# Two temporaries of the gates' exponential placed in a PSUM bank, with a newly derived instruction list

## The chip, the cores and the metric

The kernel runs on one core of a Trainium2 chip. The metric is device time in microseconds (us) of one launch, taken as the median of several runs. A core has five engines that run side by side, each strictly in its own order: TensorE (PE in the profile; its weight loads are PEld), VectorE (DVE), ScalarE (ACT), GpSimd (POOL) and SyncE (SP), which here only starts DMAs. Its two near memories are SBUF and PSUM; PSUM has eight banks of 512 float32 values in each of 128 partitions.

## The reference, cut to what matters

Two layers, one after the other. The first is a gated recurrent attention (4 batches, 8 heads, 768 steps, head size 40). Per step and head, with the running maximum `m`:

```python
m_new  = np.maximum(f_gate[t] + m, i_gate[t])
f_stab = np.exp(f_gate[t] + m - m_new)
i_stab = np.exp(i_gate[t] - m_new)
C = f_stab * C + i_stab * outer(v[t], k[t]);  n = f_stab * n + i_stab * k[t]
y[t] = sigmoid(o_gate[t]) * (C @ q[t]) / max(|n . q[t]|, 1)
```

The second is a feed-forward layer on the 3072 rows of 320 values that come out: `h = x @ w_in` (2048 columns), `g = (a0 + a1 h + a2 h^2 + a3 h^3) / (1 + |b0||h| + |b1| h^2 + 1e-6)`, `g @ w_out`. Everything is float32.

## The kernel before, in words

**The work.** Attention is cut into 24 units (6 blocks of 128 steps by 4 batches). A unit `u` loads k, q, v (`lk_u`, `lq_u`, `lv_u`), scales k by the input gate (`kp_u`, POOL), transposes k and q on TensorE (`tk_u`, `tq_u`) with copies back on ACT (`ek_u`, `eq_u`), forms the decays by a scan (`sc_u`, DVE), multiplies q by them (`qa_u`, DVE for the first ten units), and makes the score products `S_u`, the masked scores `P_u` (two DVE multiplies), the new state `ow_u`, and the state updates `u0_u`, `u1_u` (DVE). Two units make a pair `m`, whose outputs are `it_m`, `i1_m` (TensorE), `ab_m`, `rc_m`, `g_m`, `x_m`, then transposes `xt_m` and splits into a high and a low part (`xh_m` ACT, `xl_m` DVE).

The feed-forward layer runs over 12 blocks `n` of 256 rows by 8 steps `i` of 256 hidden columns. Step `n_i` is: `f1` (16 matmuls into a PSUM tile `ph`), `ha`, `p1`, `u`, `y`, `r0` (ACT), `p3`, `gh`, `m`, `gl` (DVE), `w`, `rm` (POOL), `f2` and `f3` (matmuls into `po`; `f2` needs `gh`, `f3` needs `gl`). In the trace `gh` writes the tile gH, `gl` writes gL, `m` writes w, `p3` writes p, `sc` writes e, `u0` writes sm, `u1` writes st, `P` writes pm. The weights come as 32-bit words, loaded by `raw_i*`, `raw_j*`, `raw_o*` and split on ACT (`s0`, `s2`, `o0`), DVE (`s1`, `s3`; tiles lo0i, zi, lo1o, zo and the like) and POOL (`o2`). The first two blocks run in two halves of four steps each.

**The gates.** All input and forget gates are turned into factors by an exponential that is built from arithmetic on DVE (`exp`, lines 461 to 484): a clamp, a scaling with rounding, a subtraction, two reductions, a polynomial of degree six, a shift of the exponent, a mask and a last product. A small part for the first 256 steps is done early (`early`). The rest (`gates`, lines 561 to 662) is one pass over tiles of 128 partitions by 256 values, named gate_x in the trace. Its operations carry the list names gate.7 to gate.20: gate.7 the clamp, gate.8 and gate.9 the scaling and the subtraction, gate.10 and gate.11 the reductions, gate.12 the first and gate.13 to gate.17 the other steps of the polynomial, gate.18 the shift, gate.19 the mask, gate.20 the product. All of their temporaries (t, n, r, p) lie in SBUF. Afterwards gate.22 (TensorE, tile pi), gate.24, gate.25 and some DMAs bring the factors to the units from the third block of steps on.

**The order.** The text `ORDER` (lines 147 to 309) lists every operation by name, `name.k` being the k-th operation of that name. `_Plan.listed` and `_Plan.issue` issue the operations in this order, so each engine and the DMA queue of SP run in the order in which their own operations stand there. Six of the eight PSUM banks form a ring "h" (`BANKS = 6`), which `ph`, the transposes (kq, px), scores (ps), outputs (y), states (ow) and the weights' lo tiles share; a new tile takes a bank when all users of an older tile are through. The 90 operations `hot` are matmuls whose result nobody reads; both lists have all of them ahead of f2_0_0.

Of the kernel before, what the change touches and what calls it, by code (L numbers as in the profile page):

```python
# [159 lines left out]
o2_j0 o2_j0.1 hot.68 S_1 P_1 P_1.1 s1_o3 gate.9 s3_o3.1 o2_j1.1 pf_2 ogl_1 ogl_3 og_0 ow_1 u0_1 s3_o3 gate.10 sc_2  # L160
it_0 it_0.1 i1_0 hot.69 ab_0 ab_0.1 rc_0 raw_i2 s0_i2 d1_1 u1_1 s1_i2 hot.70 hot.71 s2_i2 g_0 x_0 raw_i0 s2_i0 s0_i0
raw_i1 lk_2 gate.11 s3_i2 g_0.1 hot.72 hot.73 hot.74 hot.75 hot.76 gate.12 kp_2 raw_o2 pa_3 hot.77 hot.78 x_0.1 s0_i1
pc_3 s1_i0 hot.79 hot.80 xt_0 o0_i2 hot.81 lq_2 oc_j0 lk_3 o2_i2 s3_i0 hot.82 hot.83 hot.84 tk_2 o0_o3 lq_3 xh_0 s1_i1
o0_i0 o2_i0 lv_2 xh_0.1 xl_0 xl_0.1 gate.13 ek_2 s0_o2 s1_o2 gate.18 s2_i1 hot.85 hot.86 hot.87 hot.88 ke_2 kp_3 s3_i1
hot.89 lk_4 tq_2 s2_o2 s0_o2.1 s3_o2 eq_2 o0_i1 qa_2 s1_o2.1 f1_0_0 f1_0_0.1 S_2 tk_3 P_2 gate.14 P_2.1 pf_3 raw_i3
gate ow_2 ha_0_0 p1_0_0 u_0_0 raw_i7 ek_3 tq_3 p3_0_0 s3_o2.1 oc_j1 sc_3 o2_o3 o2_i1 w_0_0 y_0_0 lv_3 f1_0_1 eq_3
gate.19 raw_i5 u0_2 lq_4 lf_4 gate.1 d1_2 gate.15 gate.16 u1_2 qa_3 o0_o2 f1_0_1.1 S_3 ke_3 P_3 r0_0_0 gh_0_0 P_3.1
ha_0_1 s0_i3 f2_0_0 f2_0_0.1 s2_i3 u_0_1 f1_0_2 s1_i3 lq_5 o2_o2 s0_i7 m_0_0 kp_4 s3_i3 f1_0_2.1 p1_0_1 s1_i7 p3_0_1
ow_3 s2_i7 s3_i7 o0_i3 w_0_1 y_0_1 r0_0_1 rm_0_0 lk_5 gl_0_0 it_1 it_1.1 u0_3 i1_1 ha_0_2 u_0_2 o2_i3 gh_0_1 m_0_1
d1_3 u1_3 f1_0_3 f1_0_3.1 w_0_2 ab_1 ab_1.1 p1_0_2 rc_1 s0_i5 p3_0_2 f3_0_0 s2_i5 s1_i5 ha_0_3 p1_0_3 f3_0_0.1 g_1 x_1  # L170
rm_0_1 s3_i5 tk_4 ek_4 y_0_2 f2_0_1 gl_0_1 f2_0_1.1 u_0_3 g_1.1 x_1.1 xt_1 sc_4 xh_1 w_0_3 p3_0_3 tq_4 eq_4 xh_1.1
ke_4 kp_5 xl_1 xl_1.1 f3_0_1 f3_0_1.1 S_4 r0_0_2 o0_i5 raw_o4 gate.17 P_4 y_0_3 r0_0_3 o2_i5 P_4.1 f1_1_0 gh_0_2
gh_0_3 m_0_2 m_0_3 tk_5 ek_5 f1_1_0.1 ha_1_0 la_4 qa_4 s0_o4 s2_o4 s1_o4 rm_0_2 f1_1_1 o0_i7 s3_o4 gl_0_2 lv_4 lf_5
rm_0_3 sc_5 gl_0_3 s0_o4.1 u_1_0 f2_0_2 f2_0_2.1 f1_1_1.1 w_1_0 s1_o4.1 p1_1_0 ha_1_1 tq_5 p3_1_0 raw_o7 ow_4 la_5
# [5 lines left out]
f2_1_1.1 gate.20 gh_1_3 ha_0_4 ek_6 s0_o6.1 f3_1_1 f3_1_1.1 s1_o6.1 f2_1_2 f1_0_5 o0_o4 u_0_4 p1_0_4 m_1_3 gl_1_2  # L180
f1_0_5.1 lf_7 s0_o6 ha_0_5 f2_1_2.1 la_6 g_2.1 x_2.1 tq_6 s1_o6 s3_o6.1 gate.24 rm_1_3 gl_1_3 w_0_4 u_0_5 f3_1_2
f3_1_2.1 f2_1_3 w_0_5 p1_0_5 eq_6 f1_0_6 o2_o4 s3_o6 o0_o6 f1_0_6.1 p3_0_4 y_0_4 r0_0_4 o2_o6 ha_0_6 gate.25 p3_0_5
y_0_5 S_6 qa_6 P_6 f2_1_3.1 f3_1_3 f3_1_3.1 r0_0_5 lk_7 pe_1_3 s0_o7.1 pe_1_3.1 u_0_6 lv_6 lv_7 f1_0_7 f1_0_7.1 P_6.1
gh_0_4 m_0_4 rm_0_4 ha_0_7 p1_0_6 ogl_10 f2_0_4 f1_1_4 u_0_7 gh_0_5 w_0_6 m_0_5 gl_0_4 f2_0_4.1 f3_0_4 f3_0_4.1
gate.22 f2_0_5 f1_1_4.1 s1_o7.1 p3_0_6 p1_0_7 y_0_6 s3_o7.1 p3_0_7 r0_0_6 rm_0_5 gl_0_5 gate.23 o0_o7 ha_1_4 w_0_7
kp_7 f2_0_5.1 f3_0_5 xt_2 o2_o7 f3_0_5.1 gh_0_6 m_0_6 xh_2 xl_2 lq_8 gate.26 y_0_7 r0_0_7 lk_8 tk_7 f2_0_6 rm_0_6
f2_0_6.1 u_1_4 w_1_4 ek_7 f1_1_5 f1_1_5.1 f1_1_6 gh_0_7 m_0_7 gl_0_6 p1_1_4 xh_2.1 f3_0_6 p3_1_4 xl_2.1 ha_1_5 sc_7
u_1_5 y_1_4 rm_0_7 gl_0_7 f3_0_6.1 p1_1_5 r0_1_4 gh_1_4 ogl_8 ogl_6 la_7 ogl_9 lf_8 lk_9 ogl_11 ke_7 ogl_7 f2_0_7
f2_0_7.1 p3_1_5 m_1_4 f1_1_6.1 ha_1_6 u_1_6 tq_7 f1_1_7 w_1_5 w_1_6 rm_1_4 y_1_5 p1_1_6 f3_0_7 f3_0_7.1 ev_0_7
ev_0_7.1 r0_1_5 f1_1_7.1 f1_2_0 p3_1_6 gh_1_5 y_1_6 r0_1_6 ha_1_7 gate.27 f2_1_4 f2_1_4.1 m_1_5 lq_9 gl_1_4 f1_2_0.1  # L190
eq_7 f3_1_4 qa_7 f3_1_4.1 f2_1_5 ed_0_7 rm_1_5 gl_1_5 S_7 P_7 ow_6 kp_8 f2_1_5.1 d0_6 f3_1_5 tk_8 P_7.1 lk_10 p1_1_7
p3_1_7 u_1_7 gh_1_6 m_1_6 ha_2_0 u_2_0 p1_2_0 f1_2_1 f3_1_5.1 f2_1_6 p3_2_0 u0_6 w_1_7 y_1_7 r0_1_7 w_2_0 f2_1_6.1
f1_2_1.1 rm_1_6 ek_8 y_2_0 gh_1_7 d1_6 u1_6 m_1_7 d0_7 gl_1_6 rm_1_7 ow_7 u0_7 r0_2_0 it_3 it_3.1 gh_2_0 og_6 d1_7
u1_7 la_8 ogl_16 sc_8 i1_3 tq_8 ab_3 ha_2_1 m_2_0 gl_1_7 ab_3.1 p1_2_1 rm_2_0 p3_2_1 f3_1_6 f3_1_6.1 f2_1_7 u_2_1 rc_3
# [10 lines left out]
u_3_0 la_10 ed_1_7.1 lq_11 lv_10 gate.28 p3_3_0 xt_4 S_10 xh_4 P_10 f2_2_6.1 y_2_7 r0_2_7 xl_4 P_10.1 xh_4.1 f3_2_6
f3_2_6.1 gh_2_7 f1_3_1 w_3_0 kp_11 y_3_0 r0_3_0 f1_3_1.1 ha_3_1 xl_4.1 tk_11 m_2_7 gh_3_0 m_3_0 f1_3_2 f1_3_2.1 qa_10
ek_11 tq_11 f2_2_7 f2_2_7.1 rm_2_7 rm_3_0 gl_2_7 p1_3_1 u_3_1 ha_3_2 f3_2_7 f3_2_7.1 ow_10 eq_11 lq_12 lf_11 S_11
p3_3_1 w_3_1 gl_3_0 u_3_2 ev_2_7 ev_2_7.1 sc_11 ke_11 y_3_1 r0_3_1 gh_3_1 d0_10 P_11 u0_10 p1_3_2 lv_11 p3_3_2 m_3_1
f1_3_3 f1_3_3.1 ha_3_3 u_3_3 f2_3_0 p1_3_3 P_11.1 f2_3_0.1 f3_3_0 w_3_2 f3_3_0.1 f2_3_1 la_11 lf_12 kp_12 w_3_3 d1_10
# [1254 lines left out]
```

## Time and profile before

| | us |
|---|---|
| median of 3 runs (lowest, highest) | 518.59 (517.47, 518.70) |
| the profiled execution, its own time | 516.0 |
| span of its trace, first to last instruction | 514.1 |
| TensorE busy | 483.4 |
| VectorE busy | 429.8 |
| ScalarE busy | 403.7 |
| GpSimd busy | 382.6 |

Busy times are sums over the whole span. [...] What ended an engine's idle time stands in brackets behind an instruction of the timeline. An instruction that is held up after it has started shows as a long one, not as idle time.

### The profile page before, as it was taken

The numbers are of one execution on the slowest core, as the hardware profiler recorded it, in microseconds if no ns is written. First come the engines' busy times: TensorE is split into PE (matmuls) and PEld (weight loads), VectorE is DVE, ScalarE is ACT, GpSimd is POOL, SyncE is SP. The second block draws the span as 40 slices with busy tenths as digits, with TensorE's granted clock in tenths as the row PEclk, the third lists the DMA queues.
The fourth block names the chain that finished last, engine by engine and source line by source line (L and its number), as shares of the span: only waits on it lengthen the run. The fifth ranks groups of instructions, "written<-read, shape, count | busy, mean of one in ns | idle before, by whom it ended". The sixth has DMA issues, their size and how long they took to land.

```text
span 514.1 us, 14184 instructions
## 1 busy us (share of the span) xinstructions
PE 483.4 (94%) x5631; PEld 466.0 (91%) x5631; DVE 429.8 (84%) x716; ACT 403.7 (79%) x698; POOL 382.6 (74%) x365
## 2 busy tenths in 40 slices
...
GB/s 177 186 181 251 213 145 211 52 53 108 61 128 51 52 102 102 80 77 79 83 30 143 108 52 71 82 35 42 46 62 81 1 74 1 18 12 2 27 1 33
DMA packets 119439, 42.55 MB, mean 83 GB/s; under 512 B 103618, under 2 KB 111874, under 8 KB 119362
## 3 DMA queue, kind: packets, MB, share of 16 engines
...
q14 instruction: 31, 0.25, 0.2%
q10 hardware_dynamic: 130, 0.16, 0.1%
...
## 4 chain that ended last, share of the span: by engine, by line
PE 71%; DVE 9%; DMA 4%; issue 4%; ACT 4%; POOL 3%; SPq 2%; DVEq 0%; ACTq 0%; POOLq 0%
PE ph L34 28%; PE po L34 27%; PE y L34 4%; PE kq L34 3%; PE ow L34 3%; PE ps L34 3%; DVE w L34 2%; SPq L34 2%; DMA rawi<-in_moe_w_in_dram 2%; POOL p L34 2%; DVE gH L34 2%; PE px L34 1%; DMA qn<-in_q_dram 1%; PE hot L34 1%; DVE gL L34 1%
## 5 line engine op out<-in xcount | busy, mean ns | idle before, releaser
L34 POOL TENSOR_TENSOR p<-p,w 128x512 f32<-128x512 f32 (+1 forms) x97 | 126.6, 1305 | 63.4 <-DVE w L34 60.4
L34 PE MATMUL ph<-xk,wi 128*128 128x256 f32 x1152 | 169.4, 283 | 0.6 <-DVE pm L34 0.3
L34 PEld LDWEIGHTS ph<-xk,wi 128*128 128x128 f32 x1152 | 151.0, 190 | 2.4 <-issue 0.6
L34 PE MATMUL po<-wo,gH 128*128 128x320 f32 x768 | 136.6, 314 | 4.4 <-DVE gH L34 4.4
L34 POOL TENSOR_TENSOR w<-w,ha 128x512 f32<-128x512 f32 (+1 forms) x97 | 128.6, 1330 | 14.0 <-ACT w L34 13.8
L34 PEld LDWEIGHTS po<-wo,gH 128*128 128x128 f32 x768 | 116.7, 190 | 5.4 <-DVE gH L34 4.6
L34 DVE SCALAR_TENSOR_TENSOR w<-w,gH 128x512 f32<-128x512 f32 (+1 forms) x97 | 85.0, 877 | 4.5 <-POOL gt L34 0.5
L34 DVE SCALAR_TENSOR_TENSOR gL<-p,ps,ph 128x512 fp32r<-128x512 f32 (+1 forms) x97 | 71.1, 733 | 18.9 <-POOL p L34 16.7
L34 ACT ACTIVATE ph<-w,cd 128x512 f32<-128x512 f32 (+1 forms) x97 | 66.5, 687 | 23.4 <-POOL w L34 10.9
L34 DVE SCALAR_TENSOR_TENSOR gH<-p,ps,ph 128x512 fp32r<-128x512 f32 (+1 forms) x97 | 71.3, 735 | 14.7 <-ACT ph L34 12.3
L34 ACT ACTIVATE w<-ha,ba 128x512 f32<-128x512 f32 (+1 forms) x97 | 78.6, 811 | 3.1
L34 PE MATMUL po<-wo,gL 128*128 128x320 f32 x384 | 78.5, 317 | 1.1 <-DVE gL L34 1.1
L34 DVE SCALAR_TENSOR_TENSOR p<-p,ps,ph 128x512 f32<-128x512 f32 (+1 forms) x97 | 70.4, 734 | 9.9 <-ACT p L34 9.5
L34 ACT ACTIVATE ha<-ph 128x512 f32<-128x512 f32 (+1 forms) x97 | 57.6, 593 | 26.8 <-PE ph L34 25.8
L34 ACT ACTIVATE p<-ph,ps 128x512 f32<-128x512 f32 (+1 forms) x97 | 65.3, 677 | 1.5 <-DVE gL L34 1.4
L34 PEld LDWEIGHTS po<-wo,gL 128*128 128x128 f32 x384 | 59.7, 189 | 3.2 <-DVE gL L34 2.5
L34 ACT ACTIVATE ph<-ph 128x512 f32<-128x512 f32 (+1 forms) x97 | 56.1, 579 | 2.2
L34 PE MATMUL ph<-xk,wY 128*128 128x256 f32 x192 | 53.8, 280 | 0.0
L34 PE MATMUL ph<-xk,wj 128*128 128x256 f32 x192 | 53.7, 280 | 0.0
L34 PEld LDWEIGHTS ph<-xk,wj 128*128 128x128 f32 x192 | 36.4, 190 | 0.0
L34 PEld LDWEIGHTS ph<-xk,wY 128*128 128x128 f32 x192 | 36.4, 189 | 0.0
L34 PE MATMUL hot<-ident 128*128 128x128 f32 x180 | 24.8, 292 | 4.0 <-DVE flag_out L369 4.0
...
## 6 DMA issues: line engine op xcount, KB each, us to landing
...
```

Source lines behind the costliest of these rows:

```text
L34: made = fn(*args, **kwargs)
```

## The change

In `gates`, the temporaries n and p of the exponential move from SBUF into one PSUM bank of the ring "h", in columns 0 to 255 and 256 to 511. The bank is taken at gate.8, the first to write n, and comes free after gate.20, the last to read p. `exp` takes these two as functions, so that the tile is made when the first operation is issued; `early` keeps its SBUF temporaries.

```diff
     def exp(step, tiles, to=None, w=None):
-        x, t, m, r, p = tiles.values()
+        x, t, m_, r, p_ = tiles.values()
+        m, p = (z if callable(z) else lambda z=z: z for z in (m_, p_))
...
-        step(lambda: V.tensor_scalar(p, m, MAGIC, None, op0=ALU.subtract), r=[gm], w=[gp], cost=0.4)
+        step(lambda: V.tensor_scalar(p(), m(), MAGIC, None, op0=ALU.subtract), r=[gm], w=[gp], cost=0.4)
...
-        work = dict(zip(("gB.t", "gB.n", "gB.r", "gB.p"), work))
+        def bank(j):
+            if "gP" not in G:
+                G["gP"] = ring(psH, "h", [P, 512], "gP")
+            return G["gP"][:, j * 2 * SQ : (j + 1) * 2 * SQ]
+        work = {"gB.t": work[0], "gP.n": lambda: bank(0), "gB.r": work[2], "gP.p": lambda: bank(1)}
...
         def step(fn, cost=0.59, engine="DVE", w=(), r=(), **kw):
+            if "gP.n" in w:
+                kw["new"] = [("gP", ("h", BANKS))]
             plan.add("gate", engine, cost, fn, r=r, w=w, **kw)
```

The list has the same 2723 words in another order. It is the same up to word 150, and TensorE's order is the same again from f1_0_6 on, apart from a few places late in the list. Two stretches of DVE's own order, without what is left out at "...":

```
before: gate.7 s1_o3.1 gate.8 P_1 P_1.1 s1_o3 gate.9 ... gate.10 sc_2 ... gate.11 s3_i2 gate.12 ... gate.13 s1_o2 gate.18
        ... P_2 gate.14 P_2.1 p3_0_0 s3_o2.1 sc_3 gate.19 u0_2 gate.15 gate.16 u1_2 qa_3 P_3 gh_0_0 ... gate.17 ... gate.20
after:  ... P_1 P_1.1 qa_1 sc_2 u0_1 u1_1 ... qa_2 ... P_2 P_2.1 ... sc_3 gate.7 u1_2 p3_0_0 P_3 P_3.1 s1_i3 s3_i3 u0_3 qa_3
        gh_0_0 ... s3_o7 gate.8 gate.9 gate.10 gl_0_2 u0_4 sc_5 gate.11 qa_5 u1_4 gh_0_3 p3_1_0 P_5 P_5.1 gate.12 m_0_3 gate.18
        gate.13 gh_1_0 u0_5 m_1_0 gl_0_3 gate.14 u1_5 gate.15 p3_1_1 gl_1_0 gate.16 sc_6 ... gate.19 ... gate.17 ... gate.20
```

And of TensorE's and the DMA queue's:

```
PE before: f1_0_0 f1_0_0.1 S_2 tk_3 pf_3 ow_2 tq_3 f1_0_1 f1_0_1.1 S_3 f2_0_0 f2_0_0.1 f1_0_2 f1_0_2.1 ow_3 it_1 it_1.1 i1_1
PE after:  S_2 hot.84 f1_0_0 ... tk_3 ow_2 pf_3 tq_3 pa_3 S_3 f1_0_1 ow_3 it_1 it_1.1 i1_1 f1_0_1.1 f2_0_0 f2_0_0.1 tk_4 f1_0_2
SP before: ... lk_4 raw_i3 gate raw_i7 oc_j1 lv_3 raw_i5 lq_4 lf_4 gate.1 lq_5 lk_5 raw_o4 la_4 lv_4
SP after:  ... gate lv_2 lq_3 raw_i3 lv_3 lk_4 oc_j1 raw_i7 raw_o4 gate.1 lf_4 lq_4 raw_i5 lf_5 la_4
```

## Rows read from the trace of the kernel before

**Rows 1.** Windows, all engines: stretch, length, busy per engine, granted clock, DMA

```profile
40.00:60.00 20.00, 18.84 (x320) 17.26 (x320) 19.29 (x39) 18.09 (x33) 14.51 (x16) 1.00 1.00 242
...
80.00:100.00 20.00, 18.42 (x262) 17.08 (x262) 19.86 (x32) 16.19 (x30) 15.81 (x16) 0.98 0.51 110
...
120.00:460.00 340.00, 339.41 (x3970) 330.34 (x3969) 285.51 (x448) 278.74 (x477) 272.11 (x252) 1.00 0.30 66
```

**Rows 2.** Timeline of PE, 64 to 72 and 94 to 102 us

```profile
64.30 2.50 PE L34 MATMUL po<-wo,gH 128*128 128x320 f32 x8 [4.44 <-DVE gH L34]
66.60 1.48 PE L34 MATMUL ph<-xk,wi 128*128 128x256 f32 x6
...
68.30 0.88 PE L34 MATMUL ph<-xk,wi 128*128 128x256 f32 x6
...
69.34 0.79 PE L34 MATMUL ow<-vb,pm 128*64 128x82 f32 x16
...
71.80 0.96 PE L34 MATMUL ph<-xk,wi 128*128 128x256 f32 x6
...
82.71 1.33 PE L34 MATMUL po<-wo,gH 128*128 128x320 f32 x8
...
96.88 0.79 PE L34 MATMUL y<-vb,pm 128*64 128x82 f32 x16 [1.58 <-DVE gL L34]
...
99.83 1.62 PE L34 MATMUL ph<-xk,wi 128*128 128x256 f32 x6
```

**Rows 3.** Windows, same columns, where the clock fell

```profile
64.00:66.00 2.00, 1.70 (x6) 1.70 (x7) 2.00 (x4) 2.00 (x4) 1.29 (x1) 0.50 0.87 147
...
100.00:102.00 2.00, 2.00 (x10) 2.00 (x11) 1.97 (x6) 1.53 (x3) 2.00 (x3) 0.50 0.68 113
```

**Rows 4.** Timeline of DVE, 57 to 64 us

```profile
57.98 0.40 DVE L34 SCALAR_TENSOR_TENSOR gate_x<-gate_x 128x256 f32<-128x256 f32 x1
58.30 0.32 DVE L34 COPY sm<-ow 104x164 f32<-104x164 f32 x1
58.54 3.88 DVE L34 SCALAR_TENSOR_TENSOR gate_x<-gate_x 128x256 f32<-128x256 f32 x2
62.34 0.31 DVE L34 TENSOR_TENSOR st<-tm,ow 104x164 f32<-104x164 f32 x1
...
63.51 0.73 DVE L34 SCALAR_TENSOR_TENSOR gH<-p,ps,ph 128x512 fp32r<-128x512 f32 x1
```

**Rows 5.** Timeline of POOL and then of ACT, same stretch

```profile
58.70 0.58 POOL L34 TENSOR_TENSOR tm<-sm,ab 104x164 f32<-104x164 f32 x1 [2.02 <-DVE sm L34]
...
61.42 0.72 POOL L34 TENSOR_TENSOR kp<-kr,inat 128x320 f32<-128x320 f32 x1
...
62.69 0.63 ACT L34 ACTIVATE lo0i<-rawi 128x512 int32<-128x512 uint8 x1 [1.96 <-DVE st L34]
```

**Rows 6.** Instructions that touch gate_x: duration ns min/median/max, first and last start

```profile
L34 DVE SCALAR_TENSOR_TENSOR gate_x<-gate_x x9: 396/478/3437, 41.8 to 103.5; 128x256 f32<-128x256 f32 x9
L34 DVE TENSOR_SCALAR gate_x<-gate_x x5: 283/367/735, 37.9 to 51.4; 128x256 f32<-128x256 f32 x4, 128x256 int32<-128x256 int32 x1
L34 PE MATMUL pi<-ident,gate_x x2: 272/272/273, 119.7 to 119.9; 128*64 128x128 f32 x2
```

**Rows 7.** Groups of DVE by shape, 0 to 130 us: busy, mean ns

```profile
L34 DVE SCALAR_TENSOR_TENSOR gate_x<-gate_x 128x256 f32<-128x256 f32 x9 | 8.4, 937 | 0.1
L34 DVE SCALAR_TENSOR_TENSOR w<-w,gH 128x512 f32<-128x512 f32 x12 | 11.7, 983 | 0.4
L34 DVE SCALAR_TENSOR_TENSOR lo0i<-rawi,lo0i 128x512 int32<-128x512 int32 x8 | 5.5, 689 | 1.3 <-ACT lo0i L34 1.3
L34 DVE SCALAR_TENSOR_TENSOR lo1o<-rawo,lo1o 128x320 int32<-128x320 int32 x8 | 3.9, 488 | 1.3 <-ACT lo1o L34 1.1
L34 DVE TENSOR_TENSOR pm<-ps,e 128x256 f32<-128x256 f32 x14 | 5.5, 414 | 0.4 <-PE ps L34 0.4
```

**Rows 8.** Chain of waits, 57 to 64 us: start, length, what

```profile
57.76 4.60 DMA qn<-in_q_dram
```

More of the change, by code (lines that the diff above doesn't have):

```diff
@@ L160 @@
[L160 to L174, printed above, removed]
@@ L180 @@
[L180 to L194, printed above, removed]
@@ L205 @@
[L205 to L209, printed above, removed]
@@ new lines @@
+hot.83 xl_0.1 o2_i0 o2_j0.1 o0_i2 s2_o3 ke_2 S_2 hot.84 P_2 f1_0_0 f1_0_0.1 raw_o2 s0_o3 P_2.1 s2_o2 o2_i2 s1_o3 s3_o3
+s3_i1 hot.85 hot.86 hot.87 lk_3 kp_3 gate s0_o2.1 s0_o2 s1_o2.1 s1_o2 s3_o2 s0_o3.1 hot.88 hot.89 o0_i1 ha_0_0 o2_i1
+s1_o3.1 tk_3 ek_3 u_0_0 lv_2 ow_2 pf_3 s3_o2.1 u0_2 d1_2 s3_o3.1 w_0_0 sc_3 gate.7 ke_3 u1_2 o0_o2 lq_3 p1_0_0 tq_3
+o2_o2 eq_3 pa_3 p3_0_0 raw_i3 s2_i3 pc_3 S_3 P_3 P_3.1 s0_i3 s1_i3 s3_i3 lv_3 lk_4 f1_0_1 ow_3 u0_3 d1_3 kp_4 qa_3
+oc_j1 raw_i7 it_1 it_1.1 y_0_0 r0_0_0 gh_0_0 m_0_0 s2_i7 s0_i7 i1_1 ab_1 s1_i7 o0_i3 ab_1.1 f1_0_1.1 ha_0_1 u_0_1
@@ new lines @@
+p1_0_1 rm_0_0 raw_o4 rc_1 g_1 s3_i7 u1_3 gate.1 gl_0_0 f2_0_0 s2_o4 p3_0_1 w_0_1 lf_4 sc_4 s0_o4 s1_o4 o0_o3 x_1 o2_i3
+g_1.1 y_0_1 r0_0_1 gh_0_1 f2_0_0.1 tk_4 f1_0_2 f3_0_0 ek_4 f3_0_0.1 f1_0_2.1 s3_o4 m_0_1 rm_0_1 ke_4 lq_4 raw_i5 s0_i5
+ha_0_2 lf_5 s1_i5 s2_i5 x_1.1 u_0_2 s3_i5 w_0_2 gl_0_1 la_4 tq_4 eq_4 la_5 f1_0_3 qa_4 p1_0_2 f1_0_3.1 ha_0_3 xt_1
+lk_5 kp_5 f2_0_1 S_4 p1_0_3 p3_0_2 p3_0_3 xh_1 o2_o3 u_0_3 y_0_2 d0_4 raw_o7 lq_5 w_0_3 f2_0_1.1 P_4 xl_1 P_4.1 xh_1.1
+xl_1.1 tk_5 f3_0_1 r0_0_2 gh_0_2 s0_o7 f3_0_1.1 s1_o7 s2_o7 ek_5 o0_i5 f1_1_0 f1_1_0.1 m_0_2 lv_4 rm_0_2 s3_o7 f1_1_1
@@ new lines @@
+ow_4 gate.8 gate.9 gate.10 gl_0_2 u0_4 sc_5 gate.11 ha_1_0 p1_1_0 y_0_3 o2_i5 d1_4 u_1_0 lv_5 ke_5 w_1_0 tq_5 eq_5
+qa_5 f1_1_1.1 r0_0_3 f2_0_2 f2_0_2.1 u1_4 gh_0_3 ha_1_1 u_1_1 f3_0_2 S_5 w_1_1 p3_1_0 f3_0_2.1 o0_i7 P_5 P_5.1 gate.12
+ow_5 y_1_0 r0_1_0 m_0_3 gate.18 gate.13 gh_1_0 d0_5 u0_5 rm_0_3 m_1_0 f2_0_3 f1_1_2 raw_o6 s2_o6 p1_1_1 f1_1_2.1
+ha_1_2 gl_0_3 gate.14 d1_5 u1_5 f2_0_3.1 u_1_2 f3_0_3 gate.15 p3_1_1 y_1_1 rm_1_0 gl_1_0 gate.16 it_2 p1_1_2 it_2.1
+i1_2 ab_2 ab_2.1 r0_1_1 f3_0_3.1 f1_1_3 lk_6 lf_6 sc_6 f1_1_3.1 pe_0_3 pe_0_3.1 rc_2 w_1_2 f2_1_0 f2_1_0.1 gh_1_1
```

112 lines of the change are left out of this document (66 added, 46 removed).

## The prediction

> **What bounds the kernel now.** I first read the windows: from 120 to 460 us TensorE is busy 339.4 of 340 us at full clock, while the other engines have a sixth or more to spare [rows 1]. What happens there is paid for by TensorE's work alone, and the change touches no matmul. So the time can only move where TensorE still loses time, ahead of about 120 us, or at the end, where the order stays nearly as it is. Ahead of 120 us two engines press: the DMAs up to about 60 us (mean busy share 1.00, 242 GB/s in 40 to 60 us), and DVE (19.3 of 20 us busy there, and 19.9 of 20 in 80 to 100 us) [rows 1].
>
> Next I read TensorE's timeline for its holes. The largest is before the first `po` at 64.30 us: 4.44 us idle, ended by DVE's gH. [...] That is 1.2 + 0.6 = 1.8 us more, so this one hole costs 6.2 us. A second one stands at 96.88 us: 1.58 us idle, again ended by DVE, and a window at 0.50 of the clock behind it (2 us at half speed, 1.0 lost) [rows 2, 3]: 2.6 us.
>
> Then DVE's timeline ahead of that gH. Two exponential instructions take 3.88 us together; by the list of the tile's instructions the longest one takes 3.44 us, the shortest of the same shape 0.40 [rows 4, 6]. In the same time POOL runs four multiplications and subtractions without a hole, from 58.70 to 62.14 us [rows 5]. The DVE instruction, with both inputs in SBUF, ends when POOL's string ends. Behind it `st`, `qA`, `pm` and gH run without a break, and ACT too waits 1.96 us for that `st` [rows 4, 5].
>
> The point from which both lists run alike on TensorE is past by the two `pi` transposes (gate.22), at 119.7 us [rows 6]. The work ahead of it is the same set of operations in both; so the change is worth what those transposes come earlier or later.
>
> **The exponential itself.** Of its nine SCALAR_TENSOR_TENSOR instructions eight now have one input in PSUM; gate.19 keeps two in SBUF (it is the 0.40 us one at 57.98) [rows 4]. The nine take 9 x 0.937 = 8.4 us, the eight 8.0 [rows 7]. With one PSUM input the same size is to be seen in `pm` (0.414 us), and `lo1o`, which also writes PSUM, takes 0.488 for 320 columns, 0.689 for 512, so 1.05 ns a column and 0.42 for 256 [rows 7]. Eight at 0.42 are 3.4: 4.6 us less. The lower bound of the saving is 3.0 us (the 3.44 us instruction alone), the upper one 8.0 - 8 x 0.40 = 4.8. The four TENSOR_SCALARs that move (gate.8, 9, 12, 18) now take 0.28 to 0.74, median 0.37 [rows 6]; none with such a shape in PSUM stands in the trace, so I bound each by 0.28 and 0.49 (`lo1o`, larger) and take 0.42, nearest to `pm`: 0.2 us more in all at the median, up to 0.3 less against the collided one. I count it at zero.
>
> [...]
>
> **The stall and the order.** 3.0 us of TensorE's 4.44 us hole is that one instruction. The rest is cover by order: the new list puts ow_3, it_1 and i1_1 ahead of f2_0_0, work that in the trace takes from 69.34 to 71.80 us, 2.5 us [rows 2]. All of these need v of unit 3, whose load is moved ahead of raw_i7 and of oc_j1 in SP's queue. At the same time gate.8 to gate.16 leave the stretch ahead of gh_0_0. So I expect f2_0_0 to find gH ready, or nearly, and the whole 6.2 us to go (bounds: 3.0 if the rest of the hole and the slow clock stay, 6.2).
>
> **What is given back.** The gates have not gone; eleven of them (gate.8 to 16, 18, 19) now stand on DVE between gh_0_0 and gh_0_4, where only gate.17 and gate.20 stood, and DVE is the pressed engine there (19.9 of 20 us in one window) [rows 1]. An instruction of 0.40 to 0.42 us lets the next start after 0.32 (57.98 to 58.30 us) [rows 4], at 0.42 by the same overlap after 0.34, so the eleven take 3.7 to 4.6 us (without the overlap). In exchange P_3.1, s1_i3, s3_i3 and u0_3 (0.4 + 0.69 + 0.69 + 0.3 us by their kinds, 1.8 with the overlap) come ahead of gh_0_0 [rows 4, 7]. Net 1.9 to 2.5, I take 2.3. Behind each gate waits whatever DVE has next, the gH and gL on which f2 and f3 wait. In the trace before, the gates ran up to 62 us beside a DMA stage at a share of 1.00, where they filled DVE; that cover is gone, and this is the price of it.
>
> The sum: 6.2 - 2.3 = 3.9 us less. The profiled execution lasted 516.0 us (span 514.1, 1.9 around it) and would go to 512.1; the median of the runs is 518.6, 2.6 above it, and goes to 514.7. DVE's own account comes near: 4.6 us less collision over the whole start. The two small shifts of order late in the list (among others f1_9_3 behind f3_8_7, la_22 ahead of lq_22) I cost at nothing, since TensorE has other work on both sides; a hole there would cost its length.
>
> **The rivals.** (a) *The bank is missed.* One of six banks is away from gate.8 to gate.20. Counted in the lists from each tile's first to last user, at the places 540 to 599 all six are claimed at 41 of 60, before at 11 of 60. If an `f1` must wait for a bank that comes free by a gL that stands late on DVE, TensorE gets a hole as at 59.9 us with the slow clock behind it: 6.2 us, and the time is 514.7 + 6.2 = 520.9, slower. It decides from 3.9 us of such waits on; one hole like that at 96.88 (2.6 us) leaves 517.3. For it: DVE is that full, and both holes of the trace ended by DVE [rows 2]. Against: the list was made with the bank counted, and ranks an `f1` only behind the last user of the bank that it takes.
>
> (b) *Nothing that counts is won.* The chain of waits lays 4.60 us up to 62.36 us on a q load, not on DVE [rows 8]; if the DMAs at a share of 1.00 are the true bound up to 62 us, a freed DVE waits there, and the gates come on top later. Or the collisions go elsewhere: `w<-w,gH` with both inputs in SBUF takes 0.983 us in the mean where `lo0i` of the same columns takes 0.689 [rows 7], and POOL's work is no less. The time is 518.6 give or take 1.5. Against: the 3.44 us instruction uses nothing of q, and POOL's string ends with it [rows 5, 6]. [...]
>
> (c) *More is won.* With DVE freed of 4.6 us, the second hole closes too: another 2.6 us, 512.1. For it: it also waits for DVE. Against: the gates now stand just there.
>
> **How the numbers follow.** Forecast 514.7, 0.40, with a range of its own of 512.8 (nothing but 0.4 given back) to 516.6 (half the gain); (c) 0.14; (b) 0.21; (a) 0.25, since a list in another order can make holes at more places than I can price. A measurement of this kernel can tell 0.3%, 1.6 us, from no change. Faster by more is the forecast and (c), 0.54; within it is (b), 0.21; slower is (a), 0.25. The range goes from 510.0 (both holes gone, nothing given back: 518.6 - 8.8) to 521.0 (a); outside I leave some 0.05 below and 0.13 above.
>
> **What would show it.** Right: no exponential instruction with a PSUM input above 0.6 us; TensorE's hole before the first `po` under 1.5 us, and no half clock behind it; `pi` near 116 us, and the end earlier by the same; DVE without holes from 62 to 105 us. Wrong in the collision: long instructions of the exponential in spite of PSUM. Wrong in the order: a hole of TensorE of over 2 us between 70 and 110 us, ended by DVE, with an `f1` behind it (a). Wrong in the bound: the DMAs ending DVE's idle time between 45 and 60 us (b). If `pi` and the end move by different amounts, something late in the list counts.

## The result and the profile after

The changed kernel's median is 510.82 us (510.55 to 511.95, 4 runs) beside 518.64 for the kernel before (517.47 to 519.09, 4 runs): a ratio of 0.9893 with an interval of 0.9844 to 0.9941, so 5.5 us less, from 3.1 to 8.1. The two medians alone lie 7.8 us apart; the same kernel on a second chip (x0 below) gains 5.6 us by the ratio and 6.0 by the medians. The forecast was 3.9. The profiled execution took 511.0 us, with a span of 509.2 and a mean granted clock of TensorE of 0.984 of full speed (before: 516.0, 514.1 and 0.978). In the y group of the experiments one run of the kernel before took 508.92 us and the ratios count only those of its runs that lie within 1.5% of it, so the ratios of that group come out high, and I give its medians beside them.

I read the windows first, in the columns of [rows 1]; here those of the changed kernel:

```profile
20.00:40.00 20.00, 16.87 (x255) 15.34 (x255) 14.77 (x30) 12.45 (x22) 13.93 (x16) 0.83 1.00 211
40.00:60.00 20.00, 18.06 (x314) 16.62 (x309) 15.64 (x33) 17.21 (x33) 14.23 (x16) 1.00 0.89 207
60.00:104.00 44.00, 40.97 (x513) 36.99 (x512) 42.56 (x84) 38.49 (x70) 36.07 (x33) 1.00 0.66 147
...
64.00:66.00 2.00, 1.69 (x13) 1.43 (x11) 1.97 (x7) 1.97 (x7) 1.78 (x2) 1.00 0.87 155
...
100.00:102.00 2.00, 1.65 (x13) 1.42 (x12) 1.97 (x6) 2.00 (x5) 1.35 (x2) 1.00 0.00 0
...
120.00:460.00 340.00, 339.88 (x3971) 330.86 (x3971) 285.51 (x449) 278.98 (x477) 272.53 (x252) 1.00 0.30 65
```

Two of these stretches were not shown of the kernel before, so they stand here:

```profile
20.00:40.00 20.00, 17.89 (x293) 16.31 (x290) 17.75 (x37) 14.61 (x27) 16.54 (x17) 1.00 1.03 217
...
60.00:104.00 44.00, 37.66 (x471) 35.31 (x472) 42.78 (x70) 34.89 (x64) 32.37 (x32) 0.88 0.60 134
```

From 120 us on nothing has moved: 339.9 of 340 us, as in [rows 1]. Both windows that stood at half clock in [rows 3] are now at full clock. Between 60 and 104 us TensorE works 41.0 us at 1.00 where it worked 37.7 at a mean of 0.88. Between 20 and 60 us it is the other way round, a point I come back to. DVE's 3.7 us of relief in 40 to 60 us (15.6 against 19.3) go with the gates that left.

TensorE's timeline of the changed kernel from 60 us (start, length, what it does, and in brackets the idle time before it with what ended it):

```profile
60.80 0.79 PE L34 MATMUL ow<-vb,pm 128*64 128x82 f32 x16
...
64.36 1.33 PE L34 MATMUL po<-wo,gH 128*128 128x320 f32 x8
...
66.13 0.62 PE L34 MATMUL kq<-ident,kp 128*104 128x128 f32 x4 [0.44 <-DVE st L34]
...
70.10 0.65 PE L34 MATMUL kq<-ident,qn 128*104 128x128 f32 x4 [0.70 <-ACT kT L34]
...
76.90 0.61 PE L34 MATMUL kq<-ident,kp 128*104 128x128 f32 x4 [0.58 <-DVE pm L34]
...
82.44 0.65 PE L34 MATMUL kq<-ident,qn 128*104 128x128 f32 x4 [0.79 <-DVE gL L34]
...
91.32 1.35 PE L34 MATMUL y<-vb,pm 128*64 128x82 f32 x32
...
101.29 0.93 PE L34 MATMUL ph<-xk,wi 128*128 128x256 f32 x6 [0.35 <-DVE xn L34]
```

The first eight `po` start at the same 64 us as in [rows 2], but without a hole ahead of them, and take 1.33 us instead of 2.50. By then TensorE has also done ow_3, it_1 and i1_1 (the first line is ow_3). The second hole of [rows 2], 1.58 us ahead of a `y`, is gone as well. Small holes of 0.35 to 0.79 us have come in their place.

DVE's timeline of the changed kernel at the same place shows where the 3.88 us of [rows 4] went: before gH there is no gate. First, for comparison, the longer of those two gates in the kernel before:

```profile
58.98 3.44 DVE L34 SCALAR_TENSOR_TENSOR gate_x<-gate_x 128x256 f32<-128x256 f32 x1
```

And the changed kernel:

```profile
62.00 0.68 DVE L34 TENSOR_TENSOR qA<-kq,ab 104x512 f32<-104x512 f32 x1
...
62.60 0.74 DVE L34 SCALAR_TENSOR_TENSOR gH<-p,ps,ph 128x512 fp32r<-128x512 f32 x1
```

The long gate of the kernel before ends at 62.42 us, 0.28 us behind the end of POOL's string at 62.14; this distance comes back in the experiments.

The instructions of the changed kernel that touch gate_x or the bank (gP), with durations in ns as minimum, median and maximum, then first and last start:

```profile
L34 DVE SCALAR_TENSOR_TENSOR gP<-gP,gate_x x5: 420/428/433, 88.2 to 98.8; 128x256 f32<-128x256 f32 x5
L34 DVE SCALAR_TENSOR_TENSOR gate_x<-gP,gate_x x3: 400/419/424, 81.3 to 101.5; 128x256 f32<-128x256 f32 x3
L34 DVE TENSOR_SCALAR gP<-gate_x x2: 418/423/428, 80.4 to 86.8; 128x256 f32<-128x256 f32 x2
L34 DVE TENSOR_SCALAR gP<-gP x1: 433/433/433, 80.8 to 80.8; 128x256 f32<-128x256 f32 x1
...
L34 PE MATMUL pi<-ident,gate_x x2: 270/270/271, 115.8 to 115.9; 128*64 128x128 f32 x2
...
L34 DVE TENSOR_SCALAR gate_x<-gP x1: 417/417/417, 87.7 to 87.7; 128x256 int32<-128x256 int32 x1
L34 DVE SCALAR_TENSOR_TENSOR gate_x<-gate_x x1: 590/590/590, 95.3 to 95.3; 128x256 f32<-128x256 f32 x1
```

The eight SCALAR_TENSOR_TENSORs with one input in the bank lie between 0.400 and 0.433 us, where [rows 6] had 0.396 to 3.437. The one that kept both inputs in SBUF (gate.19) takes 0.590. `pi` comes at 115.8 us instead of 119.7, and the end 4.9 us earlier.

### The profile page after: what moved, and what is told of

It is laid out like the page before. It is cut to its first block, busy times and chain, and to the rows that moved or that the text cites. A ratio compares the mean times of both kernels' runs of the same rounds, so it can differ in the third digit from the quotient of the medians.

```text
span 509.2 us, 14188 instructions
## 1 busy us (share of the span) xinstructions
PE 482.7 (95%) x5631; PEld 464.4 (91%) x5631; DVE 421.0 (83%) x716; ACT 402.7 (79%) x698; POOL 383.7 (75%) x365
## 4 chain that ended last, share of the span: by engine, by line
PE 75%; DVE 8%; DMA 4%; issue 3%; ACT 3%; POOL 2%; SPq 1%; DVEq 0%; ACTq 0%; POOLq 0%
PE ph L34 29%; PE po L34 28%; PE kq L34 4%; PE y L34 4%; PE ow L34 3%; PE ps L34 3%; PE hot L34 2%; DMA rawj<-in_moe_w_in_dram 2%; DMA rawi<-in_moe_w_in_dram 2%; DVE w L34 1%; PE px L34 1%; DVE gH L34 1%; SPq L34 1%; DMA qn<-in_q_dram 1%; DVE gL L34 1%
## 5 line engine op out<-in xcount | busy, mean ns | idle before, releaser
L34 POOL TENSOR_TENSOR w<-w,ha 128x512 f32<-128x512 f32 (+1 forms) x97 | 126.9, 1313 | 10.0 <-ACT w L34 9.8
L34 PEld LDWEIGHTS po<-wo,gH 128*128 128x128 f32 x768 | 115.5, 188 | 0.9
L34 DVE SCALAR_TENSOR_TENSOR w<-w,gH 128x512 f32<-128x512 f32 (+1 forms) x97 | 82.3, 848 | 4.4
L34 PE MATMUL hot<-ident 128*128 128x128 f32 x180 | 27.1, 305 | 4.0 <-DVE flag_out L369 4.0
```

The source lines that it names most:

```text
L34: made = fn(*args, **kwargs)
```

## The experiments

Each group ran on a chip of its own, beside the kernel before, whose medians there were 516.63 (x), 516.56 (y) and 516.12 us (z). The diffs are excerpts; of the list they show only the words around a move. The last column is the start of the first `pi` in one profile.

| kernel | list | n and p | median (range) | ratio (interval) | `pi` |
|---|---|---|---|---|---|
| x0 changed, again | new | PSUM | 510.68 (510.07–511.61) | 0.9892 (0.9865–0.9918) | 115.5 |
| x1 | new | SBUF | 515.88 (513.82–518.09) | 0.9999 (0.9975–1.0023) | 120.3 |
| x2 | new | SBUF, bank held | 519.57 (517.22–522.19) | 1.0060 (1.0039–1.0082) | 125.7 |
| x3 | new, gates early | PSUM | 511.04 (509.83–513.52) | 0.9893 (0.9865–0.9922) | 117.5 |
| y1 | old | p in PSUM in part | 512.26 (508.98–514.41) | 0.9953 (0.9912–0.9995) | 116.2 |
| y2 | old, two gates later | SBUF | 513.38 (511.12–515.42) | 0.9997 (0.9955–1.0039) | 115.0 |
| y3 | old | no exponential | 509.64 (507.93–512.63) | 0.9924 (0.9883–0.9965) | 112.9 |
| y4 | new | no exponential | 510.33 (508.55–510.94) | 0.9923 (0.9892–0.9954) | 113.9 |
| z0 changed, third | new | PSUM | 509.63 (506.89–513.30) | 0.9876 (0.9832–0.9920) | 118.1 |
| z1 | new, bank held shorter | PSUM | 513.74 (509.95–516.47) | 0.9948 (0.9918–0.9979) | 121.2 |
| z2 | new, in two parts | PSUM | 510.96 (509.27–513.50) | 0.9910 (0.9882–0.9938) | 116.5 |
| z3 | new, late part as before | PSUM | 509.62 (507.89–511.50) | 0.9880 (0.9837–0.9924) | 116.1 |

**x0: the changed kernel again.** No edit.

> The changed kernel itself, beside the kernel before on one chip, as the mark for the runs next to it. Span about 509 us, pi transposes near 115.8 us; 5 to 8 us below the kernel before (ratio 0.985 to 0.990).

510.68 us against 516.63. The gain holds on another chip: 0.9892, so 5.6 us with an interval of 4.2 to 7.0. The forecast gain of 3.9 lies just below it. TensorE's timeline of x0:

```profile
64.29 1.33 PE L34 MATMUL po<-wo,gH 128*128 128x320 f32 x8
...
115.51 0.38 PE L34 MATMUL pi<-ident,gate_x 128*64 128x128 f32 x2
```

From the first `po` to `pi` it takes 51.2 us (51.5 in the profile above). I use this stretch below, since the place of the first `po` itself scatters: 64.36, 64.29 and, in z0, 66.84 us for one and the same kernel.

**x1: the new list with n and p in SBUF.**

```diff
-        work = {"gB.t": work[0], "gP.n": lambda: bank(0), "gB.r": work[2], "gP.p": lambda: bank(1)}
+        work = dict(zip(("gB.t", "gB.n", "gB.r", "gB.p"), work))
```

> The new list, but with all four temporaries of the exponential in SBUF as before (and so no bank held). Theory of the collision: the eight instructions again have both inputs in SBUF, stand where GpSimd is busy 16 of 18 us, and some take over 1 us; the pi transposes come 1.5 to 4 us later than the 115.8 of the changed kernel, and the end with them. Rival, the order alone: the collision before mattered only since the instruction stood in front of gh_0_0; in the new list TensorE has work in hand, pi stays within 0.7 us of 115.8 and the time within 1 us of the changed kernel, or it is better by the bank that is free again.

The order alone is worth nothing: 0.9999. The collisions have moved along with the gates. The same view as above, DVE's and POOL's timelines for one of the gates, and TensorE's timeline, all of x1:

```profile
L34 DVE SCALAR_TENSOR_TENSOR gate_x<-gate_x x9: 412/622/1509, 82.8 to 105.7; 128x256 f32<-128x256 f32 x9
L34 DVE TENSOR_SCALAR gate_x<-gate_x x5: 269/479/1261, 58.3 to 89.8; 128x256 f32<-128x256 f32 x4, 128x256 int32<-128x256 int32 x1
```

```profile
93.54 1.28 DVE L34 SCALAR_TENSOR_TENSOR gate_x<-gate_x 128x256 f32<-128x256 f32 x1
...
93.25 1.29 POOL L34 TENSOR_TENSOR p<-p,w 128x512 f32<-128x512 f32 x1
```

```profile
65.26 1.33 PE L34 MATMUL po<-wo,gH 128*128 128x320 f32 x8
...
86.41 0.69 PE L34 MATMUL ps<-qT,kT 40*64 40x64 f32 x30 [1.64 <-DVE qA L34]
...
88.34 1.64 PE L34 MATMUL ow<-vb,pm 128*64 128x82 f32 x16 [0.76 <-POOL w L34]
...
107.15 0.62 PE L34 MATMUL kq<-ident,kp 128*104 128x128 f32 x4 [1.50 <-DVE zo L34]
```

The hole before the first `po` is gone here too, so the order does fill it. But three holes of 0.8 to 1.6 us stand later, amid gates of up to 1.5 us, and `pi` comes 4.8 us later than in x0: 1.0 of it stands at the first `po`, 3.8 behind it (55.0 us against 51.2). All seven two-input gates of x1 above 0.5 us end 0.28 to 0.29 us behind the end of a POOL instruction, as the one shown does (94.82 and 94.54).

**x2: the same, with the bank held and not used.**

```diff
-        work = {"gB.t": work[0], "gP.n": lambda: bank(0), "gB.r": work[2], "gP.p": lambda: bank(1)}
+        work = {"gB.t": work[0], "gP.n": work[1], "gB.r": work[2], "gP.p": work[3]}
```

> As the run with the new list and temporaries in SBUF, but with one bank of the ring still kept from gate.8 to gate.20, unused. Against the changed kernel it differs by the place of the temporaries alone, against the SBUF run by the bank alone. Theory of the collision: slower than the changed kernel by 1.5 to 4 us, and within 0.5 us of the SBUF run without the bank. Rival, the bank is missed: the run without the bank is faster than this one by up to 1.8 us, the three holes of TensorE in front of kq (0.44, 0.58, 0.79 us) that end by DVE.

519.57 us, 3.7 over x1, where the theory had 0.5 at most and the rival 1.8. TensorE's timeline of x2, then DVE's and POOL's:

```profile
83.99 0.65 PE L34 MATMUL kq<-ident,qn 128*104 128x128 f32 x4 [2.28 <-DVE gL L34]
...
98.08 1.22 PE L34 MATMUL y<-vb,pm 128*64 128x82 f32 x16 [2.14 <-DVE st L34]
```

```profile
94.53 3.16 DVE L34 SCALAR_TENSOR_TENSOR gate_x<-gate_x 128x256 f32<-128x256 f32 x1
97.62 0.31 DVE L34 TENSOR_TENSOR st<-tm,ow 104x164 f32<-104x164 f32 x1
...
96.69 0.72 POOL L34 TENSOR_TENSOR kp<-kr,inat 128x320 f32<-128x320 f32 x1
```

The stall of the kernel before is here again, 36 us later: one gate of 3.16 us that ends 0.28 us behind the third of three POOL instructions in a row (97.69 and 97.41), the `st` behind it, and a hole of 2.1 us on TensorE that this `st` ends. How much of the 3.7 us is the bank and how much this one collision, one profile does not tell.

**x3: new list, gates early as in the old one, in PSUM.** The gates stand again before gh_0_0.

```diff
-ow_4 gate.8 gate.9 gate.10 gl_0_2 u0_4 sc_5 gate.11 ha_1_0
+ow_4 gl_0_2 u0_4 sc_5 ha_1_0
...
+ab_0.1 gate.7 gate.8 gate.9 u1_1 s1_i0 gate.10 gate.11 gate.12 gate.18 rc_0
+... g_0.1 gate.13 ... s0_o2 gate.14 gate.15 ... s3_o2.1 gate.19 ... w_0_0 gate.16 ... S_3 gate.17 P_3 P_3.1 gate.20
```

> The changed kernel with the exponential moved ahead in the list, into places where DVE idles in the changed kernel: gate.7 to 9 ahead of u1_1 (1.03 us idle), gate.10, 11, 12, 18 ahead of rc_0 (1.39), gate.13 ahead of x_0.1 (0.24), gate.14 and 15 ahead of s1_o2.1 (0.53), gate.16 ahead of sc_3 (0.28), 19 ahead of u0_2, 17 and 20 around P_3. The bank is free again before 62 us. Theory (DVE is the pressed engine from 64 to 101 us, and the eleven gates there cost 1.9 to 2.5 us): pi 1 to 2.5 us earlier than 115.8, no more than the 3.0 us of small holes that TensorE still has from 64 to 116 us. Rival, TensorE alone bounds that stretch and the holes have other causes: pi within 0.5 us of 115.8. Second rival: the early places delay attention units 2 and 3, f2_0_0 starts later than 64.4 us, and the time is longer.

511.04 us: no difference from x0. TensorE's timeline of x3:

```profile
47.92 0.62 PE L34 MATMUL kq<-ident,qn 128*104 128x128 f32 x4 [2.50 <-ACT lo0i L34]
...
67.65 1.33 PE L34 MATMUL po<-wo,gH 128*128 128x320 f32 x8
```

The first `po` comes 3.3 us later than in the changed kernel, with no hole directly ahead of it but one of 2.50 us further up, and `pi` only 1.7; the theory had it 1 to 2.5 earlier. From the first `po` to `pi` it is 49.9 us, 1.3 less than in x0; why is not shown, since y4 below, with no exponential at all, has the 51.2 of x0. With the two temporaries in PSUM it makes no measurable difference in which of these two places the gates stand.

**y1: the old list, p in PSUM from gate.12 to gate.16.** A tile gQ of the same ring; n and the rest of p stay in SBUF.

```diff
-        step(lambda: V.tensor_scalar(p, r, POLY[-1], None, op0=ALU.mult), r=[gr], w=[gp], cost=0.4)
-        for c in POLY[-2::-1]:
+            step(lambda: V.tensor_scalar(pq(), r, POLY[-1], None, op0=ALU.mult), r=[gr], w=["gQ"], cost=0.4)
+            for c in POLY[-2:1:-1]:
...
+                lambda c=POLY[1]: V.scalar_tensor_tensor(p, pq(), c, r, op0=ALU.add, op1=ALU.mult), r=[gr, "gQ"],
```

> The kernel before, old list, with one temporary in a PSUM bank for five instructions only: gate.12 writes p there, gate.13 to 15 work on it, gate.16 brings it back to SBUF; the bank is held from gate.12 to gate.16. Order unchanged. Theory of the collision: none of the four SCALAR_TENSOR_TENSORs gate.13 to 16 is above 0.5 us, TensorE's hole before the first po falls from 4.44 us by 3 us to about 1.4, and the time by 3 us, or by 4.8 if the clock then stays up. Rival, the transfers bound that place (the chain names a q load): the hole stays above 3 us with DVE idle, and the time is that of the kernel before within 1 us.

512.26 us, 4.3 less than the median before (2.4 by the ratio, 0.3 to 4.5), with no word of the list moved. The timeline of TensorE, and the instructions that touch gQ, both of y1:

```profile
62.41 1.44 PE L34 MATMUL po<-wo,gH 128*128 128x320 f32 x8 [1.17 <-DVE gH L34]
...
93.44 0.79 PE L34 MATMUL y<-vb,pm 128*64 128x82 f32 x16 [1.62 <-DVE gL L34]
```

```profile
L34 DVE SCALAR_TENSOR_TENSOR gQ<-gQ,gate_x x3: 414/422/422, 50.8 to 59.6; 128x256 f32<-128x256 f32 x3
...
L34 DVE SCALAR_TENSOR_TENSOR gate_x<-gQ,gate_x x1: 424/424/424, 60.1 to 60.1; 128x256 f32<-128x256 f32 x1
```

The four that stood at the stall take 0.42 us, the hole shrinks from 4.44 to 1.17, and the second hole stays at 1.62.

**y2: the old list, gate.15 and gate.16 behind u1_3, all in SBUF.**

```diff
-lf_4 gate.1 d1_2 gate.15 gate.16 u1_2 qa_3
+lf_4 gate.1 d1_2 u1_2 qa_3
...
-d1_3 u1_3 f1_0_3
+d1_3 u1_3 gate.15 gate.16 f1_0_3
```

> The kernel before with two words of the list moved: gate.15 and gate.16 stand behind u1_3 instead of ahead of u1_2; temporaries in SBUF as before. Theory (what counts is the collision in front of gh_0_0): the hole of 4.44 us falls by about 3.9 us, less what other DVE instructions now collide; the two gates cost 0.8 us later, or more if they collide there; time 2 to 4.5 us below the kernel before. Rival, only the PSUM operand helps: the collision goes along to the new place, and the time is within 1 us of the kernel before.

513.38 us, 3.2 less by the medians; the ratio, which comes out high, gives no difference. TensorE's timeline of y2:

```profile
60.79 1.44 PE L34 MATMUL po<-wo,gH 128*128 128x320 f32 x8 [1.16 <-DVE gH L34]
...
71.07 0.62 PE L34 MATMUL kq<-ident,kp 128*104 128x128 f32 x4 [1.92 <-DVE xn L34]
```

Moving the two instructions out of POOL's string closes the first hole as far as PSUM does in y1, and lengthens the one ahead of this `kq`, where they now stand, from 0.32 us to 1.92; the longest gate is 1.44 us. That the order can avoid this one collision is shown; that it avoids all of them is not.

**y3 and y4: gate.8 to gate.20 left out,** with the old list and with the new one (where the bank is still claimed). The condition in the diff keeps gate.7 alone; the exponential is not computed in either.

```diff
-        exp(lambda fn, r, w, **kw: step(fn, r=halves_of(r), w=halves_of(w), **kw), dict(gx=x, **work))
+        exp(lambda fn, r, w, **kw: step(fn if w == ["gB.t"] and r == ["gx"] and kw.get("cost") else (lambda: None), r=halves_of(r), w=halves_of(w), **kw), dict(gx=x, **work))
```

> The kernel before without gate.8 to gate.20: the exponential of the gates after the first 256 steps is left out (the factors are the raw differences). Gives all that the exponential costs in the old list. Theory: the hole with its slow clock (3.0 to 4.8 us), and what its last two instructions cost at 79 and 103 us, 0.5 to 1: 3.5 to 6 us below the kernel before. Rival, more than the hole: its other instructions up to 55 us delay what follows too; 6 to 9 us.

> The changed kernel without gate.8 to gate.20 (the same part left out, the bank still kept). Gives what the exponential still costs in the new list. Theory (eleven of them cost 1.9 to 2.5 us where DVE is pressed): pi 2 to 3 us earlier than the 115.8 of the changed kernel. Rival, TensorE has work in hand there: 0 to 1 us.

509.64 and 510.33 us. So the thirteen instructions cost 6.9 us in the kernel before (516.56 - 509.64; 3.9 by the ratio of that group), 5.6 with the new list and SBUF (515.88 - 510.33, across two chips whose medians of the kernel before agree within 0.1), and 0.4 in the changed one (510.68 - 510.33, across the same two). Without the exponential the two lists differ by 0.7 us, the old one ahead, well within their ranges: the new order is worth something only together with the exponential. By `pi`, in one profile each, the thirteen are 6.4 us in x1 and 1.6 in x0 against y4:

```profile
62.65 1.33 PE L34 MATMUL po<-wo,gH 128*128 128x320 f32 x8
...
113.87 0.38 PE L34 MATMUL pi<-ident,gate_x 128*64 128x128 f32 x2
```

But in y4 the first `po` stands 1.6 us ahead of that of x0, and from there to `pi` it takes the same 51.2 us. So the 1.6 us lie wholly ahead of the first `po`, where in the new list none of the thirteen stands: behind it they cost the changed kernel nothing that these profiles can show, and x1 3.8 us. In the kernel before the nine of [rows 7] last 8.4 us together, and the slow clock behind the stall comes on top, so the 6.9 us are not simply their length. And y3, with the old list, leaves 1.19 us of the first hole: that part is the order's.

**z0: the changed kernel a third time,** to stand beside the z group.

> The changed kernel a third time, as the mark for the three runs next to it on this chip: 510 to 512 us, pi between 115 and 116 us.

509.63 us, 0.9876. `pi`, expected at 115 to 116 us, stands at 118.1, all of it from a later first `po` (66.84 us); from there it is 51.2 us again.

**z1: the bank held shorter.** gate.8 to gate.11 directly before gate.12; gate.17 and gate.20 directly behind gate.19.

```diff
-P_5 P_5.1 gate.12 ow_5
+P_5 P_5.1 gate.8 gate.9 gate.10 gate.11 gate.12 ow_5
...
-p1_1_3 gate.19 m_1_1
+p1_1_3 gate.19 gate.17 gate.20 m_1_1
```

> The changed kernel with the bank held for less of the list: gate.8 to 11 move down to stand directly ahead of gate.12, gate.17 and gate.20 move up directly behind gate.19. Without the exponential but with the bank kept, pi stood at 113.9 us; with the bank kept and SBUF temporaries 125.7 against 120.3 without the bank. Theory, the bank still costs TensorE in the changed kernel: the hole of 0.8 to 0.9 us ahead of tq_5 closes, pi 0.5 to 1.5 us earlier. Rival, the bank costs only where long collisions hold it: pi within 0.4 us, the time the same.

513.74 us, 4.1 slower than z0, against both theory and rival: the bank was held for less and the time rose. TensorE's timeline of z1, and the windows behind it:

```profile
93.50 0.56 PE L34 MATMUL po<-wo,gL 128*128 128x320 f32 x2 [1.69 <-DVE gL L34]
```

```profile
94.00:96.00 2.00, 2.00 (x33) 1.91 (x32) 2.00 (x6) 0.97 (x2) 2.00 (x3) 0.58 0.03 8
96.00:98.00 2.00, 2.00 (x69) 1.84 (x65) 1.34 (x2) 0.33 (x1) 0.26 (x1) 0.50 0.15 23
98.00:100.00 2.00, 2.00 (x13) 2.00 (x10) 1.46 (x5) 1.66 (x5) 0.72 (x1) 0.50 0.70 106
100.00:102.00 2.00, 2.00 (x14) 2.00 (x14) 1.97 (x6) 0.14 (x1) 0.48 (x1) 0.71 0.72 117
```

With the gates packed, a gL stands behind them and TensorE idles 1.69 us for it. Then these four windows are granted 0.58, 0.50, 0.50 and 0.71 of the clock, 3.4 us of full speed lost (0.8 + 1 + 1 + 0.6). That is 5.1 us. On the other side the hole that the changed kernel has at 82.44 us, ahead of tq_5, did close, as the theory had it: 0.8 us. The rest, 4.3, is about the loss, by the medians and from the first `po` to `pi` (55.4 us against 51.2 in z0). The spread of the gates is worth more than the bank.

**z2: the exponential in two parts.** gate.7 to gate.11 and gate.18 early, gate.12 to gate.17, gate.19 and gate.20 in the late place, p in a second tile gR. The diff is against the changed kernel and leaves out the moves in the list.

```diff
-        step(lambda: V.tensor_scalar(p(), r, POLY[-1], None, op0=ALU.mult), r=[gr], w=[gp], cost=0.4)
+        step(lambda: V.tensor_scalar(q(), r, POLY[-1], None, op0=ALU.mult), r=[gr], w=[gq], cost=0.4)
```

> The changed kernel with the exponential in two parts, each with its own PSUM tile: gate.7 to 11 and 18 early, in idle places of DVE (ahead of rc_0, x_0.1 and s1_o2.1, bank given back by about 54 us), gate.12 to 17, 19 and 20 late (bank from gate.12, gate.17 and 20 directly behind gate.19). Theory, the part on DVE from 64 to 101 us is what the exponential still costs (1.7 to 2.0 us of pi): six of twelve instructions gone from there give 0.8 to 1.2 us. Rival, as in the run with all of it early: the early part delays units 2 and 3 and the first po by as much, no gain, or longer by up to 1 us.

510.96 us, 1.3 over z0 in a group whose z0 itself ranges over 6 us: no difference that can be told, where the theory had 0.8 to 1.2 less.

**z3: the part of the list behind `pi` as before.**

```diff
-rm_3_1 ha_3_4 gl_3_1 gh_3_3 f1_3_5 d0_11 rm_3_2 gl_3_2
+rm_3_1 ha_3_4 gh_3_3 f1_3_5 d0_11 rm_3_2 gl_3_1 gl_3_2
...
```

> The changed kernel with the part of the list behind the last load of the start (all that lies behind the pi transposes) put back as before; the start as changed. Of the 4.9 us of span, 3.9 stood at pi and 1.0 came behind it (0.5 between the tenth and eleventh px transposes, 0.25 near 210 us). Theory, the late shifts bring that: 0.5 to 1.0 us longer than the changed kernel, the tenth to eleventh px 38.3 us apart as before against 37.9. Rival, the late part follows from the state in which the start leaves the engines: no difference above 0.3 us.

509.62 us, the same as z0; with six runs each, spread over 4 to 6 us, the medians alone could not tell the 0.5 to 1.0 us of the theory. The profile can: from `pi` to the end z3 takes 393.6 us, the changed kernel 393.4, the kernel before 394.4. Putting the late part back does not bring the 1.0 us back, which is the rival's reading. Of the kernels with the exponential none here is faster than the changed kernel by more than the runs can tell.

## Why the prediction was right, and where its sizes were off

The measured 510.82 us lies below the forecast's own range (512.8 to 516.6), nearest to rival (c) at 512.1. The mechanism of the gain was right; the sizes of its terms were not, and what was to be given back came from another cause.

**The collision: right, and shown.** x1 against x0 differs by the place of n and p (and the bank) alone, on one chip: 5.2 us by the medians. The long gates of the kernel before, of x1 and of x2 all end 0.28 to 0.29 us behind a POOL instruction; with one input in PSUM none is long (0.433 us at most). The prediction's "ends when POOL's string ends" holds for the two longest; others end behind the first of several.

**The first hole and its clock (6.2 us to go): both went, 4.3 us came of it.** The 6.2 us are 4.44 of idle time and 1.8 of the clock: behind the hole, where 0.50 of full speed was granted [rows 3], eight `po` take 2.50 us against 1.33 of later ones and six `ph` 1.48 against 0.88 [rows 2]. The first `po` starts no earlier than before (64.36 against 64.30). What was won is the 2.5 us of work now done ahead of it and the 1.8 us of the clock. The other 1.9 us of the hole were lost again further up (see `pi` below). On how the hole closes, 3.0 for the collision and the rest for the order was half of the story. y1 takes the collision alone away and gets 3.3 us of the hole, x1 takes the order alone and gets all of it, and yet x1 gains nothing: the collisions strike elsewhere. What the old list would give with both n and p in PSUM was not run; y1 comes nearest, with p for five instructions, and is 1.6 us over x0 by medians of two chips. Rival (b), nothing won, has one half of its reason right ("the collisions go elsewhere"), which holds for SBUF alone. Its other half, that the DMAs set the time up to 62 us, does not hold for this hole: in y1, y2 and y3 it shrinks to 1.16 to 1.19 us, and the first `po` comes 1.9 to 4.5 us earlier than at 64.30 (the same kernel scatters by 2.5 us there).

**The exponential (eight at 0.42 us): right,** 0.400 to 0.433. The four TENSOR_SCALARs at 0.42 too. Against the 0.396 us of the shortest with both inputs in SBUF in [rows 6] it is 4 to 37 ns more. For TENSOR_SCALAR the step is larger: 0.417 to 0.433 in PSUM against 0.283 at least in [rows 6]. Over all runs, of the two-input gates none with one input in PSUM took more than 0.433 us, those with two SBUF inputs up to 3.44. More was freed than these: the four TENSOR_SCALARs that move, counted at zero, were held up in SBUF as well, with a single input, up to 0.735 us in [rows 6] and 1.261 in x1, and in PSUM took 0.433 at most.

**What is given back (2.3 us): the gates give back nothing that shows.** Beside a kernel without the exponential the changed one loses 0.4 us by the medians, and from the first `po` to `pi` nothing (51.2 us in x0 and y4). DVE is as full as I said, 42.6 of 44 us between 60 and 104, but an instruction of a known 0.42 us fits between two pieces of work whose results are not due. I counted DVE's time as TensorE's time.

**The second hole (2.6 us, taken to stay): gone.** That is rival (c), which I gave 0.14. It stays at 1.62 us in y1, with the old list, and in y3, with the old list and no exponential, so its end is the new order's doing and not that of a freed DVE, as (c) had it. Most of it came back: the five small holes of TensorE after 64 us in the timeline above and one of 0.17 near 115 us add up to 3.0 us, where the kernel before, by the same view, had 2.35 after its first `po` (0.32, 1.58, 0.28 and 0.17; the 1.58 stands in [rows 2]). Without the second hole that is 2.3 us more, the size of the term "given back", but by luck: y4, without the gates, has 3.5 us of such holes, so they are the new list's. `w<-w,gH`, the example of rival (b) for collisions elsewhere, still has long ones, but shorter: from 0.679 up to 1.151 us, before from 0.679 up to 1.898. Its group, DVE by shape from 0 to 130 us in the changed kernel, is at a mean of 768 ns, where [rows 7] has 983:

```profile
L34 DVE SCALAR_TENSOR_TENSOR w<-w,gH 128x512 f32<-128x512 f32 x13 | 10.0, 768 | 0.5
```

**`pi` near 116 us: right to a tenth (115.8), but by luck.** Between 20 and 60 us the changed kernel lost something that no step priced: TensorE works 1.8 us less there (34.9 against 36.7), and 20 to 40 us is granted 0.83 instead of 1.00. With it goes a wait of 3.13 us for a q load at 25 us, 0.47 before. In all profiles with the new list that wait is 1.7 to 3.1 us, with the old one 0.5 to 1.8. How much of the early wait is the list's and how much chance stays open.

**The bank (rival a): not missed, though it may have a price.** With slow gates x2 is 3.7 us over x1, where the rival put 6.2, and a longer collision is in it. In the three profiles of the changed kernel TensorE's holes behind the first `po` stay under 1 us, and holding the bank for less makes it worse (z1).

**Span 4.9 against `pi` 3.9:** the last 1.0 us lies behind `pi`, and it is no scatter. From `pi` to the end the four profiles with the old list (before, y1, y2, y3) take 393.9 to 394.4 us, nine of the ten with the new list 393.4 to 393.6; x3, with the gates early, takes 394.2. z3 shows that the shifts of order late in the list are not its cause. So it goes with the start, and what of the start does it stays open.

Added up from the rows: 4.3 of the first hole, 2.6 of the second, less 2.3 of small holes, is 4.6 us, where `pi` shows 3.9 in one profile each; the 0.7 between them stays open. The forecast's 6.2 - 2.3 came to the same 3.9 with a first term too large, a second with another cause, and one left out. By the three ratios (0.9893, 0.9892, 0.9876) the result is 5.5 to 6.4 us instead of 3.9.
